# Two MLPs behind a decay attention: the second product into C11 ahead of U2's copy, and the first weights and gate tiles made sooner

## The chip, the core and the metric

The kernel runs on one core of a Trainium2 chip. The metric is the device time of one execution in microseconds (us). The engines of the core work at the same time, each through its own instructions in order: TensorE (PE; its weight loads are PEld), VectorE (DVE), ScalarE (ACT), GpSimd (POOL), and SyncE (SP), whose queue issues nearly all transfers here.

## The reference

```python
def _attn_ref(q, k, v, lam):          # 2 x 8 heads, 768 positions, 64 wide, in blocks of 64
    for b in range(nb):
        intra = np.einsum('bhic,bhjc->bhij', qb, kb) * Dmask[None]
        intra = np.einsum('bhij,bhjd->bhid', intra, vb)
        inter = np.einsum('bhid,bhde->bhie', qb * lam_pow[None], kv_state)
        out[:, :, sl] = intra + inter
        kv_state = lam_block * kv_state + np.einsum('bhsd,bhse->bhde', kb * rev_pow, vb)

def _moe_ref(x, w_in, w_out):         # x 1536 x 512, w_in 512 x 2048, w_out 2048 x 512
    h = x @ w_in
    return (h * np.cos(h)) @ w_out

def _moe2_ref(x, w_in, w_out):
    h = x @ w_in
    return (h * (1.0 / (1.0 + np.exp(-h)))) @ w_out
# out = moe2(moe(attention))
```

## The kernel before, in words

Three kinds of stage follow each other. **Attention** goes over six chunks of 128 positions (`c` 0 to 5) and leaves its result, transposed and already combined as the next stage wants it, in `xah`/`xal` (part A, the first 512 positions of both batches) and `xbh`/`xbl` (part B, the last 256). Then come, for layer 1 and again for layer 2, **the expansion** `gemm_in` (x @ w_in and the activation) and **the contraction** `gemm_out`/`gemm_outs` (@ w_out).

Every fp32 operand is split in two: `split` makes `hi` (a rounded copy, on ACT) and `lo` (the rest, `of - hi`, on POOL unless an engine is named). A product is made of hi*hi, lo*hi and hi*lo.

The expansion uses a scheme with seven products in place of eight. A *quad* is two row tiles of the hidden layer by two token halves; there are 16 per layer, eight of part A (512 columns) and eight of part B (256), in the order AA BB AB AB AB AB AA BB. `product(Q, i)` is six matmuls into one of three PSUM banks: products 1 and 2 into bank a (C11), 6, 5 and 3 into bank b, 7 and 4 into `d`. Banks a and b are the two halves of one tile, `cab`. Between them ACT copies: `copy_ab` (a to b after product 1), `copy_u(.., "u2")` (b after product 6, which is U2), `copy_u(.., "u4")` (b after product 5). DVE makes `h2` of d, u2 and u4 (`c22`, `c21`); ACT and DVE make the activation (`act_n`, `act_s`, `act_sin`, `act_g`; layer 2 needs only `act_n` and `act_g`), and SP stores the gate to DRAM (`gd`). The code is scheduled by hand: what is written order is each engine's order. The loop of `gemm_in` is skewed: round n starts quad n+1 (products 1, 7, 6, 2) and finishes quad n (5, 3, 4). Waits between engines are kept per tile.

In each round two numbered slots (2n and 2n+1) run `task`s, which prepare weights: `rebias_w` (ACT), `convert_w` (DVE), `load_next` (SP), `sum_w` (four sums of weights, POOL), `split_plain` and `split_sums`. For a pair of tiles they are `pair_tasks`; `w`, the converted tile, has four buffers. The last slots make the first w_out pieces (`out_tasks`), load the first gate tiles back (`load_g`) and split them (`prepare`).

The contraction goes over 16 hidden tiles f for three token blocks b: b = 0 and 1 interleaved, then b = 2. Its first matmuls stand in the last round of the expansion. While b = 2 of layer 1 runs, `keep_a` combines and splits the results of b = 0 and 1 as layer 2's part A, and layer 2's first two pairs of weights are made.

Of the kernel before, what the change touches and what calls it, by code (L numbers as in the profile page):

```python
# [8 lines left out]
F32 = mybir.dt.float32  # L9
# [4 lines left out]
ALU = mybir.AluOpType  # L14
PSUM = bass.MemoryType.PSUM
# [24 lines left out]
def tile_decay_attention__two_mlps(  # L40
# [84 lines left out]

    def sum_w(L, j):
        (wa0, wb0), (wa1, wb1) = (
            (w32[L, f, 0][:, 0:2 * P], w32[L, f, 0][:, 2 * P:]) for f in (2 * j, 2 * j + 1)
        )
        s = conv.tile([P, 4, 2 * P], F32, tag="S", name="S")  # L130
        for i, (x, y, op) in enumerate(
            ((wa1, wb1, ALU.add), (s[:, 0], wa0, ALU.subtract), (wa0, wa1, ALU.subtract), (wb0, s[:, 1], ALU.subtract))
        ):
            nc.gpsimd.tensor_tensor(out=s[:, i], in0=x, in1=y, op=op)  # L134
        sums[L, j] = s
# [19 lines left out]

    def pair_tasks(L, j):
        f = 2 * j
        return [
            lambda: rebias_w(L, f, 0),
            lambda: (rebias_w(L, f + 1, 0), convert_w(L, f, 0), load_next()),  # L160
            lambda: (convert_w(L, f + 1, 0), load_next(), sum_w(L, j)),
            lambda: split_plain(L, j),
            lambda: split_sums(L, j),
        ]
# [27 lines left out]
    )  # L192
    ps_o, ps_s = (psum_up.enter_context(tc.tile_pool(name=n, bufs=1, space=PSUM)) for n in ("ps_o", "ps_s"))
    half = [slice(e * C, (e + 1) * C) for e in range(2)]
# [181 lines left out]
    def att_l(c):  # L376
        h, l, ps, xc, t = xs.pop(c)
        nc.scalar.copy(h[:, 3:7], t)
        engine = nc.gpsimd if c < CA - 1 else nc.vector
        for o, x in ((slice(0, 2), xc[:, 0]), (2, xc[:, 1, 1])):  # L380
            engine.tensor_tensor(out=l[:, o], in0=x, in1=h[:, o].bitcast(F32), op=ALU.subtract)
        nc.gpsimd.tensor_tensor(out=l[:, 3:7], in0=t, in1=h[:, 3:7].bitcast(F32), op=ALU.subtract)

# [90 lines left out]
    def gemm_in(L, tasks, begun):  # L474

        qs = quads[L]

        def task(i):
            for x in tasks.get(i, []):
                x()  # L480

        if not begun:
            late = keep_b()
            late.pop(0)()
            product(qs[0], 1)
            copy_ab(qs[0])
            product(qs[0], 7)
            late.pop(0)()
            product(qs[0], 6)
            copy_u(qs[0], "u2")  # L490
            product(qs[0], 2)
            for i, x in enumerate(late):
                tasks.setdefault(i // 2, []).append(x)
        for n, Q in enumerate(qs):
            nxt = qs[n + 1] if n + 1 < len(qs) else None
            old = qs[n - 1] if n else None
            if nxt:
# [12 lines left out]
            if nxt:  # L510
                product(nxt, 7)
                product(nxt, 6)
            else:
                gemm_out(L, 0, 0, (0, 1))
            if old:
                act_g(old, 1)
            if nxt:
                copy_u(nxt, "u2")
            task(2 * n + 1)
            if nxt:  # L520
                product(nxt, 2)
# [29 lines left out]

    def prepare(L, b, f):
        if f >= FT or (L, b, f) in gt:
            return
        t = gf.pop((L, b, f))
        if b == 0:
            if L not in slab:
                slab[L] = [xpool.tile([P, SLOTS, 2, TB], F32R, tag=n, name=m) for n, m in (("xah", "gh"), ("xal", "gl"))]
            gh, gl = (x[:, f % SLOTS] for x in slab[L])
            split(gh, gl, t)  # L560
            for i in range(2):
                gt[L, i, f] = gh[:, i], gl[:, i]
        else:
            gh = tpool.tile([P, TB], F32R, tag="t2", name="gh", bufs=5)
            gl = tpool.tile([P, TB], F32R, tag="u", name="gl", bufs=3)
            split(gh, gl, t)
            gt[L, b, f] = gh, gl
# [36 lines left out]
    def keep_a():  # L604
# [65 lines left out]
    def gemm_outs(L, tasks):  # L670
# [3 lines left out]
        for b, f in items:  # L674
# [5 lines left out]
            if b == 1 and f >= FT - 4:  # L680
                load_g(L, 2, 2 * (f - FT + 4))
                if f >= FT - 2:
                    prepare(L, 2, f - FT + 2)
            if b == 2:
                if f >= 2 and f % 2 == 0:
                    load_g(L, 2, f + 4)
                prepare(L, 2, f + 2)
# [9 lines left out]
    with tc.manual_schedule():  # L697
# [29 lines left out]
        for c in range(SC):  # L727
# [31 lines left out]
            if c == 3:  # L759
                p0[0]()  # L760
            if c == 4:
                p0[1]()
            if c == 5:
                p0[2]()
# [4 lines left out]
                p0[3]()  # L769
            att_intra(c - 1)  # L770
# [5 lines left out]
        att_scores(c, 0, ps_s, "s")  # L776
        p0[4]()
        p1[0]()
        att_t(c - 1)
        product(first, 1)  # L780
        copy_ab(first)
        att_scores(c, 1, ps_s, "s")
        p1[1]()
        att_l(c - 1)
        product(first, 2)
        att_inter(c, ps_o, "o")
        product(first, 7)
# [20 lines left out]
        for L in range(2):  # L808
            tasks = {}
            for j in range(2, FP):  # L810
                place(tasks, min(4 * j - 8, 18), pair_tasks(L, j))
            for f, n in enumerate((20, 22, 24, 25, 26, 28, 29)):
                place(tasks, n - 1, out_tasks(L, f))
            for f, (n, m) in enumerate(((28, 29), (28, 30), (30, 31), (30, 32))):
                tasks.setdefault(n, []).append(lambda L=L, f=f: load_g(L, 0, f))
                if m < 32:
                    tasks.setdefault(m, []).append(lambda L=L, f=f: prepare(L, 0, f))
            gemm_in(L, tasks, L == 0)
# [4 lines left out]
            if L == 0:  # L823
# [43 lines left out]
```

## Time and profile before

| | |
|---|---|
| time, median of 3 runs | 654.67 us (650.4 to 656.73) |
| the profiled execution | 654.53 us, of which the span is 652.6 us |
| busy share of the span | PE 90%, DVE 55%, ACT 47%, POOL 55% |
| mean granted TensorE clock | 0.961 of full speed |
| TensorE's waits for ACT's copies u | 34.9 us in 32 waits |

A row of a trace gives the start and length of an operation (or a group of equal ones, `x4`), its output and inputs by the program's names, and in square brackets how long its engine stood idle before it and what ended that. L410 is the line of `product`, L432 that of `copy_u`, L121 and L122 the two halves of `split`, L591 the contraction.

### The profile page before, as it was taken

What the parts mean: (1) busy time and instruction counts of PE and PEld (TensorE: products, weight loads), DVE (VectorE), ACT (ScalarE), POOL (GpSimd) and SP (SyncE); (2) the same over time, 40 slices, a digit from 0 to 9 for tenths busy, and PEclk for the clock granted to TensorE, in tenths of its full rate; (3) what the DMA queues carried; (4) which work ended last, traced back from release to release, by engine and by line L of the source; (5) the groups of instructions that cost most, each with busy time, mean ns of one, the idle gap of its engine ahead of it and who ended that gap; (6) DMA issues with size and microseconds to landing.
All of it is one profiled execution on the core that took longest, in us unless ns stands there. A gap on an engine that the chain in (4) does not pass through costs nothing.

```text
span 652.6 us, 8744 instructions
## 1 busy us (share of the span) xinstructions
PE 586.1 (90%) x3313; PEld 482.2 (74%) x3313; DVE 360.8 (55%) x387; ACT 307.8 (47%) x482; POOL 356.1 (55%) x267
## 2 busy tenths in 40 slices
PE   7997887888788879999998998888889799999996
PEld 4876676777667768888886777777768688888884
DVE  5677766576786766960194046565676479502101
ACT  4565456666667465530364265554565455301210
POOL 3676724355372258990279635455672689821441
PEclk9998997898979779999998999999999799999999
DMA  9995234244343558771115015344555787304401
GB/s 180 211 215 141 65 130 133 93 162 160 131 161 130 195 209 283 247 247 43 34 55 172 0 33 209 115 161 159 180 190 194 277 289 260 96 1 138 157 29 64
DMA packets 79225, 97.04 MB, mean 149 GB/s; under 512 B 40784, under 2 KB 57168, under 8 KB 79184
## 3 DMA queue, kind: packets, MB, share of 16 engines
q1 hardware_dynamic: 76944, 95.96, 45.9%
q10 hardware_dynamic: 2240, 0.53, 0.4%
q8 instruction: 26, 0.43, 0.3%
q14 instruction: 15, 0.12, 0.1%
HBM read 68.16 MB, written 28.31 MB: 148 GB/s over the span
## 4 chain that ended last, share of the span: by engine, by line
PE 67%; ACT 11%; POOL 6%; DVE 5%; DMA 5%; issue 3%; SPq 1%; ACTq 0%; POOLq 0%; DVEq 0%
PE y L591 37%; PE cab L410 21%; PE d L410 8%; ACT u L432 3%; ACT s L465 2%; DMA v<-in_v_dram 2%; POOL win L122 2%; POOL S L134 2%; ACT win L121 2%; ACT s L449 2%; POOL gl L122 1%; DMA gf<-gd 1%; DVE w L116 1%; DMA q<-in_q_dram 1%; DVE sb L115 1%
## 5 line engine op out<-in xcount | busy, mean ns | idle before, releaser
L122 POOL TENSOR_TENSOR gl<-gf,gh 128x1024 fp32r<-128x1024 f32 (+1 forms) x64 | 122.4, 1918 | 98.6 <-ACT gh L121 73.9
L591 PE MATMUL y<-wout,gh 128*128 128x512 f32 x384 | 119.7, 394 | 4.0 <-ACT gh L121 2.3
L591 PE MATMUL y<-gh,wout 128*128 128x512 f32 x384 | 120.5, 396 | 2.2 <-ACT gh L121 2.2
L410 PE MATMUL cab<-xah,win 128*128 128x512 f32 x320 | 93.8, 416 | 14.3 <-ACT u L432 11.7
L116 DVE SCALAR_TENSOR_TENSOR w<-w,sb 128x512 uint32<-128x512 uint32 x64 | 90.3, 1411 | 20.0 <-ACT w L106 14.0
L121 ACT CAST gh<-gf 128x1024 fp32r<-128x1024 f32 (+1 forms) x64 | 52.9, 831 | 98.6 <-PE y L591 35.8
L591 PEld LDWEIGHTS y<-wout,gh 128*128 128x128 f32 x384 | 72.5, 190 | 19.6 <-ACT gh L121 2.6
L591 PEld LDWEIGHTS y<-gh,wout 128*128 128x128 f32 x384 | 73.5, 192 | 17.4 <-ACT gh L121 2.4
L410 PEld LDWEIGHTS cab<-xah,win 128*128 128x128 f32 x320 | 59.1, 196 | 32.5 <-ACT u L432 18.5
L134 POOL TENSOR_TENSOR S<-w 128x256 f32<-128x256 f32 x32 | 33.8, 1056 | 87.8 <-DVE w L116 87.8
L591 PE MATMUL y<-gl,wout 128*128 128x512 f32 x192 | 76.7, 399 | 5.5 <-POOL gl L122 5.5
L410 PE MATMUL cab<-xbh,win 128*128 128x256 f32 x320 | 57.1, 303 | 26.3 <-ACT u L432 23.2
L591 PE MATMUL y<-wout,gl 128*128 128x512 f32 x192 | 75.8, 395 | 1.7 <-POOL gl L122 1.7
L122 POOL TENSOR_TENSOR wout<-w,wout 128x512 fp32r<-128x512 f32 x32 | 50.8, 1589 | 42.0 <-ACT wout L121 42.0
L410 PEld LDWEIGHTS cab<-xbh,win 128*128 128x128 f32 x320 | 48.7, 201 | 33.4 <-ACT u L432 26.5
L115 DVE TENSOR_SCALAR sb<-raw 128x512 uint32<-128x512 uint32 x64 | 67.8, 1059 | 0.7
L122 POOL TENSOR_TENSOR win<-S,win 128x512 fp32r<-128x512 f32 x32 | 45.8, 1452 | 15.8 <-ACT win L121 15.8
L440 DVE TENSOR_TENSOR h<-d,u 128x512 f32<-128x512 f32 (+1 forms) x32 | 17.8, 556 | 64.7 <-PE d L410 64.7
L410 PE MATMUL cab<-xal,win 128*128 128x512 f32 x160 | 51.5, 404 | 0.0
L666 DVE COPY o<-y 128x512 f32<-128x512 f32 x12 | 8.1, 689 | 77.3 <-PE y L591 75.1
L591 PEld LDWEIGHTS y<-gl,wout 128*128 128x128 f32 x192 | 36.7, 191 | 15.1 <-POOL gl L122 7.4
L106 ACT ACTIVATE w<-raw 128x512 f32<-128x512 f32 x64 | 42.8, 669 | 7.8 <-POOL win L122 7.8
(113 smaller groups left out, 926.4 us busy)
## 6 DMA issues: line engine op xcount, KB each, us to landing
gf<-gd SPq DMA_DIRECT2D x48, 512.0 KB, 4.7
raw<-in_moe_w_in_dram SPq DMA_DIRECT2D x32, 512.0 KB, 3.9
gd<-s SPq DMA_DIRECT2D x32, 512.0 KB, 2.9
raw<-in_moe_w_out_dram SPq DMA_DIRECT2D x32, 512.0 KB, 3.5
gd<-s SPq DMA_DIRECT2D x32, 256.0 KB, 2.0
v<-in_v_dram SPq DMA_DIRECT2D x12, 256.0 KB, 6.5
out_dram<-o SPq DMA_DIRECT2D x12, 256.0 KB, 2.0
k<-in_k_dram SPq DMA_DIRECT2D x6, 256.0 KB, 6.0
```

What stands on the lines that cost most here:

```text
L106: nc.scalar.activation(w, raw[piece][:, :, 1].bitcast(F32), AF.Prelu, scale=2.0**-112, alpha=-(2.0**32))
L115: nc.vector.tensor_scalar(out=sb, in0=r[:, :, 0], scalar1=2.0**-29, scalar2=7.0, op0=ALU.mult, op1=ALU.min)
L116: nc.vector.scalar_tensor_tensor(out=w, in0=w, scalar=3, in1=sb, op0=ALU.logical_shift_left, op1=ALU.bitwise_or)
L121: nc.scalar.copy(hi, of)
L122: (engine or nc.gpsimd).tensor_tensor(out=lo, in0=of, in1=hi.bitcast(F32), op=ALU.subtract)
L134: nc.gpsimd.tensor_tensor(out=s[:, i], in0=x, in1=y, op=op)
L410: nc.tensor.matmul(Q.banks[bank], w[:, part, wu, kt * P:(kt + 1) * P], x[:, xu, kt, :], start=start and m == 0 and kt == 0, stop=m == 2 an ...
L432: nc.scalar.copy(t, Q.banks["b"])
L440: nc.vector.tensor_tensor(out=Q.h2[:, 0], in0=Q.banks["d"], in1=Q.u2, op=ALU.add)
L449: nc.scalar.activation(t, source(Q, i), AF.Identity, scale=1.0 / (2.0 * math.pi), bias=quarter)
L465: nc.scalar.activation(t, t, AF.Sin, scale=2.0 * math.pi, bias=half_pi)
L591: nc.tensor.matmul(y[m], x, z, start=f == 0 and n == 0, stop=f == FT - 1 and n == 2)
```

## The change

In `gemm_in`, `product(nxt, 2)` is written before `copy_u(nxt, "u2")`. `load_g(L, 0, 0)` goes to the head of round 14, and the first three gate tiles are split in two pieces (`prepare(.., 2)`). At the end of the attention the first weights are converted one chunk sooner, summed and split ahead of x's lo; x's lo of chunk 3 goes to POOL, that of chunks 4 and 5 reads PSUM, and a late part of it is issued after the second pair's sums. The two PSUM pools `ps_o` and `ps_s` change places. At the end of layer 1's contraction all four subtractions of `rest` and the sums of weights run on DVE, the weights' tasks start at f = 0, and the gate loads of b = 2 stand one step later at first and then two steps ahead. Loop counts, arithmetic and tile sizes stay.

```diff
-    def sum_w(L, j):
+    def sum_w(L, j, engine):
...
-    def pair_tasks(L, j):
+    def pair_tasks(L, j, engine=nc.gpsimd):
...
-            lambda: (convert_w(L, f + 1, 0), load_next(), sum_w(L, j)),
+            lambda: (convert_w(L, f + 1, 0), load_next()),
+            lambda: sum_w(L, j, engine),
...
-        engine = nc.gpsimd if c < CA - 1 else nc.vector
-        for o, x in ((slice(0, 2), xc[:, 0]), (2, xc[:, 1, 1])):
+        engine, x = (nc.gpsimd, xc) if c < CA else (nc.vector, ps)
+        for o, x in ((slice(0, 2), x[:, 0]), (2, x[:, 1, 1])):
             engine.tensor_tensor(out=l[:, o], in0=x, in1=h[:, o].bitcast(F32), op=ALU.subtract)
...
             product(qs[0], 6)
+            product(qs[0], 2)
             copy_u(qs[0], "u2")
-            product(qs[0], 2)
...
+            if n == len(qs) - 2:
+                load_g(L, 0, 0)
             if nxt:
                 product(nxt, 1)
...
             if nxt:
+                product(nxt, 2)
                 copy_u(nxt, "u2")
             task(2 * n + 1)
-            if nxt:
-                product(nxt, 2)
             product(Q, 3)
...
             for i in range(2):
                 gt[L, i, f] = gh[:, i], gl[:, i]
+                if pieces == 2:
+                    split(*gt[L, i, f], t[:, i])
+            if pieces == 1:
+                split(gh, gl, t)
...
-            split(h[:, 3 + i], l[:, 3 + i], t[i], nc.vector if i % 2 else nc.gpsimd)
+            split(h[:, 3 + i], l[:, 3 + i], t[i], nc.vector)
...
             if b == 2:
-                if f >= 2 and f % 2 == 0:
-                    load_g(L, 2, f + 4)
+                if f % 2 == 0:
+                    load_g(L, 2, f + 6)
...
+            if c == 5:
+                p0[3]()
+                p0[4]()
             if c > 1:
                 att_l(c - 2)
...
-                for j, ns in enumerate(((3, 4, 5, 7, 8), (8, 9, 10, 11, 12))):
-                    for n, x in zip(ns, pair_tasks(1, j)):
+                for j, ns in enumerate(((0, 1, 2, 3, 7, 8), (4, 5, 6, 9, 10, 12))):
+                    for n, x in zip(ns, pair_tasks(1, j, nc.vector)):
```

TensorE in a middle round of layer 1, before: product 6 of a part A quad (`cab_1226`), its product 2, and product 3 of the part B quad ahead of it (`cab_1149`).

```order
L410 MATMUL cab_1226<-xah_309,win_1119 128x512 [waits Activation_49]
L410 MATMUL cab_1226<-xah_309,win_1119 128x512 x3
L410 MATMUL cab_1226<-xal_310,win_1119 128x512 x2
L410 MATMUL cab_1226<-xah_309,win_1119 128x512 [waits Activation_49]
L410 MATMUL cab_1226<-xah_309,win_1119 128x512 x3
L410 MATMUL cab_1226<-xal_310,win_1119 128x512 x2
L410 MATMUL cab_1149<-xbh_836,win_962 128x256 x4
L410 MATMUL cab_1149<-xbl_837,win_962 128x256 x2
```

The same three products in the changed kernel.

```order
L414 MATMUL cab_1226<-xah_309,win_1125 128x512 [waits Activation_49]
L414 MATMUL cab_1226<-xah_309,win_1125 128x512 x3
L414 MATMUL cab_1226<-xal_310,win_1125 128x512 x2
L414 MATMUL cab_1226<-xah_309,win_1125 128x512 x4
L414 MATMUL cab_1226<-xal_310,win_1125 128x512 x2
L414 MATMUL cab_1149<-xbh_836,win_961 128x256 [waits Activation_49]
L414 MATMUL cab_1149<-xbh_836,win_961 128x256 x3
L414 MATMUL cab_1149<-xbl_837,win_961 128x256 x2
```

Product 2 waits for nothing now, and the wait for an ACT copy stands at product 3, whose copy is u4.

SP at the end of layer 1's expansion, before: stores of the gate, a load of raw weights, and the first two gate tiles (`gf`).

```order
L472 DMA gd0_74<-s_2032 128x1024 [waits DVE_49]
L472 DMA gd0_74<-s_2100 128x1024 [waits DMAHW3_49,DVE_49]
L92 DMA raw_2138<-in_moe_w_out_dram 128x1024 [waits DMAHW4_49,DMAHW5_49,DVE_49,Activation_49]
L545 DMA gf_2142<-gd0_74 128x1024 [waits DMAHW2_49,PE_49]
L545 DMA gf_2144<-gd0_74 128x1024 [waits DMAHW6_49,DVE_49]
```

The same place after.

```order
L476 DMA gd0_74<-s_2032 128x1024 [waits DVE_49]
L550 DMA gf_2113<-gd0_74 128x1024 [waits DMAHW3_49,DMAHW2_49,PE_49]
L476 DMA gd0_74<-s_2100 128x1024 [waits DMAHW4_49,DVE_49]
L92 DMA raw_2140<-in_moe_w_out_dram 128x1024 [waits DMAHW5_49,DVE_49,Activation_49]
L550 DMA gf_2144<-gd0_74 128x1024 [waits DMAHW6_49,DVE_49]
```

The first gate tile is two entries further ahead in the queue; the second stays where it was.

POOL where the attention ends, as a difference: lo of the first pair's plain weights, lo of x (`xal`, `xbl`), and lo of the sums.

```order
 L122 TENSOR_TENSOR win<-w,win 128x512
 L122 TENSOR_TENSOR win<-w,win 128x256
+L382 TENSOR_TENSOR xal<-xc,xah 128x4x128
+L382 TENSOR_TENSOR xal<-xc,xah 128x2x128
+L383 TENSOR_TENSOR xal<-xt,xah 128x8x128
 L122 TENSOR_TENSOR win<-S,win 128x512 x2
-L382 TENSOR_TENSOR xbl<-xt,xbh 128x8x128
 L134 TENSOR_TENSOR S<-w 128x256
```

The weights' lo now stands ahead of x's lo of chunk 3, and one lo of part B goes behind the second pair's sums.

## Rows read from the trace of the kernel before

**Rows 1.** Busy time by stretch: start:end, length, PE, PEld, DVE, ACT, POOL, clock, DMA, GB/s.

```profile
82.00:223.00 141.00, 116.61 (x590) 98.09 (x589) 94.53 (x118) 92.17 (x146) 58.86 (x53) 0.92 0.40 138
223.00:240.00 17.00, 12.80 (x54) 10.72 (x55) 10.84 (x13) 8.00 (x14) 8.18 (x5) 0.70 0.83 279
...
372.00:504.00 132.00, 118.93 (x640) 99.50 (x639) 78.61 (x99) 74.25 (x132) 65.75 (x57) 1.00 0.43 150
504.00:519.00 15.00, 10.70 (x51) 8.80 (x52) 6.89 (x9) 6.24 (x10) 9.38 (x5) 0.77 0.84 297
327.00:372.00 45.00, 41.16 (x173) 33.25 (x172) 23.11 (x16) 19.34 (x31) 40.35 (x31) 0.96 0.26 82
```

**Rows 2.** Waits, whole span: waiting engine <- releaser: us, times, longest.

```profile
PE cab L410 <- ACT u L432: 34.9, 32, 3.3
...
ACT u L432 <- PE cab L410: 23.1, 22, 2.3
```

**Rows 3.** Chain that ended last, layer 2: start, length of one product (x6).

```profile
392.03 0.73 PE d L410 x6
...
437.10 1.36 PE d L410 x6
```

**Rows 4.** Timeline of TensorE, layer 2: product 2 of three successive quads.

```profile
443.95 1.19 PE L410 MATMUL cab<-xah,win 128*128 128x512 f32 x4 [0.68 <-ACT u L432]
...
451.75 0.74 PE L410 MATMUL cab<-xbh,win 128*128 128x256 f32 x4 [1.16 <-ACT u L432]
...
460.95 1.19 PE L410 MATMUL cab<-xah,win 128*128 128x512 f32 x4 [0.68 <-ACT u L432]
```

**Rows 5.** Timeline of TensorE, layer 1: product 2 of two part B quads.

```profile
140.47 0.74 PE L410 MATMUL cab<-xbh,win 128*128 128x256 f32 x4 [1.77 <-ACT u L432]
...
158.05 0.74 PE L410 MATMUL cab<-xbh,win 128*128 128x256 f32 x4 [1.76 <-ACT u L432]
```

**Rows 6.** Busy time in one pair of quads of layer 1.

```profile
140.00:158.00 18.00, 15.15 (x84) 12.91 (x84) 13.01 (x17) 13.04 (x23) 9.43 (x10) 1.00 0.42 146
```

**Rows 7.** Groups in 82 to 223: count, busy, mean ns, idle before them, releaser.

```profile
L449 ACT ACTIVATE s<-h,consts 128x1024 int32<-128x1024 f32 x8 | 9.2, 1153 | 9.5 <-DVE h L440 9.5
...
L440 DVE TENSOR_TENSOR h<-d,u 128x512 f32<-128x512 f32 x8 | 5.5, 692 | 21.2 <-PE d L410 21.2
...
L428 ACT COPY cab<-cab 128x256 f32<-128x256 f32 x8 | 2.9, 366 | 0.0
```

**Rows 8.** Timeline, layer 1, around 175 us.

```profile
175.31 0.67 ACT L106 ACTIVATE w<-raw 128x512 f32<-128x512 f32 x1 [4.71 <-POOL win L122]
...
177.49 0.74 PE L410 MATMUL cab<-xbh,win 128*128 128x256 f32 x4 [2.32 <-ACT cab L428]
```

**Rows 9.** Timeline at the passage from expansion to contraction, layer 1, then 2.

```profile
229.03 1.04 ACT L121 CAST gh<-gf 128x1024 fp32r<-128x1024 f32 x1 [4.50 <-DMA gf<-gd]
...
230.13 0.73 PE L591 MATMUL y<-gh,wout 128*128 128x512 f32 x2 [2.17 <-ACT gh L121]
...
232.57 0.79 PE L591 MATMUL y<-gl,wout 128*128 128x512 f32 x1 [1.71 <-POOL gl L122]
...
509.74 0.73 PE L591 MATMUL y<-wout,gh 128*128 128x512 f32 x2 [2.35 <-ACT gh L121]
```

**Rows 10.** Timeline of SP and TensorE late in layer 1's contraction.

```profile
340.28 0.96 SPq L548 DMA_DIRECT2D gf<-gd  x2
...
348.77 0.50 PE L591 MATMUL y<-gl,wout 128*128 128x512 f32 x1 [3.23 <-POOL gl L122]
```

**Rows 11.** Timeline of TensorE at the end of the attention.

```profile
61.82 0.73 PE L410 MATMUL cab<-xah,win 128*128 128x512 f32 x2 [2.17 <-POOL win L122]
...
79.59 0.73 PE L410 MATMUL d<-xah,win 128*128 128x512 f32 x2 [0.31 <-POOL win L122]
```

**Rows 12.** Timeline of DVE, end of layer 1: two subtractions of one size.

```profile
323.05 1.23 DVE L596 TENSOR_TENSOR T<-y,x 128x1024 f32<-128x1024 f32 x1 [35.49 <-ACT b L613]
...
327.01 2.30 DVE L596 TENSOR_TENSOR T<-x,T 128x1024 f32<-128x1024 f32 x1
```

More of the change, by code (lines that the diff above doesn't have):

```diff
@@ L133, in sum_w @@
         ):
-            nc.gpsimd.tensor_tensor(out=s[:, i], in0=x, in1=y, op=op)
+            engine.tensor_tensor(out=s[:, i], in0=x, in1=y, op=op)
         sums[L, j] = s
@@ L192, in tile_decay_attention__two_mlps @@
     )
-    ps_o, ps_s = (psum_up.enter_context(tc.tile_pool(name=n, bufs=1, space=PSUM)) for n in ("ps_o", "ps_s"))
+    ps_s, ps_o = (psum_up.enter_context(tc.tile_pool(name=n, bufs=1, space=PSUM)) for n in ("ps_s", "ps_o"))
     half = [slice(e * C, (e + 1) * C) for e in range(2)]
@@ L378, in att_l @@
         nc.scalar.copy(h[:, 3:7], t)
-        engine = nc.gpsimd if c < CA - 1 else nc.vector
-        for o, x in ((slice(0, 2), xc[:, 0]), (2, xc[:, 1, 1])):
+        engine, x = (nc.gpsimd, xc) if c < CA else (nc.vector, ps)
+        for o, x in ((slice(0, 2), x[:, 0]), (2, x[:, 1, 1])):
             engine.tensor_tensor(out=l[:, o], in0=x, in1=h[:, o].bitcast(F32), op=ALU.subtract)
-        nc.gpsimd.tensor_tensor(out=l[:, 3:7], in0=t, in1=h[:, 3:7].bitcast(F32), op=ALU.subtract)
+        late = lambda: nc.gpsimd.tensor_tensor(out=l[:, 3:7], in0=t, in1=h[:, 3:7].bitcast(F32), op=ALU.subtract)
+        if c == CA:
+            return late
+        late()
     class Quad:
@@ L550, in load_g, with prepare @@
                 gf[L, 2, f + i] = t[:, i]
-    def prepare(L, b, f):
+    def prepare(L, b, f, pieces=1):
         if f >= FT or (L, b, f) in gt:
@@ L559, in prepare @@
             gh, gl = (x[:, f % SLOTS] for x in slab[L])
-            split(gh, gl, t)
             for i in range(2):
                 gt[L, i, f] = gh[:, i], gl[:, i]
+                if pieces == 2:
+                    split(*gt[L, i, f], t[:, i])
+            if pieces == 1:
+                split(gh, gl, t)
         else:
@@ L680, in gemm_outs @@
             if b == 1 and f >= FT - 4:
-                load_g(L, 2, 2 * (f - FT + 4))
+                if f >= FT - 3:
+                    load_g(L, 2, 2 * (f - FT + 3))
                 if f >= FT - 2:
@@ L759, in tile_decay_attention__two_mlps @@
             if c == 3:
-                p0[0]()
+                rebias_w(0, 0, 0)
+                convert_w(0, 0, 0)
+                load_next()
             if c == 4:
-                p0[1]()
+                rebias_w(0, 1, 0)
+                convert_w(0, 1, 0)
+                load_next()
             if c == 5:
-                p0[2]()
                 qk_pools.close()
@@ L768, in tile_decay_attention__two_mlps @@
                 )
-                p0[3]()
             att_intra(c - 1)
@@ L776, in tile_decay_attention__two_mlps @@
         att_scores(c, 0, ps_s, "s")
-        p0[4]()
+        p0[5]()
         p1[0]()
         att_t(c - 1)
+        late = att_l(c - 1)
         product(first, 1)
@@ L783, in tile_decay_attention__two_mlps @@
         p1[1]()
-        att_l(c - 1)
         product(first, 2)
@@ L789, in tile_decay_attention__two_mlps @@
         p1[2]()
+        p1[3]()
         att_x(c)
-        p1[3]()
+        p1[4]()
         product(first, 6)
+        late()
         att_t(c)
-        p1[4]()
+        p1[5]()
         att_l(c)
@@ L810, in tile_decay_attention__two_mlps @@
             for j in range(2, FP):
-                place(tasks, min(4 * j - 8, 18), pair_tasks(L, j))
+                at_n = min(4 * j - 8, 18)
+                p = pair_tasks(L, j)
+                for n, x in zip((0, 1, 2, 2, 3, 4), p):
+                    tasks.setdefault(at_n + n, []).append(x)
             for f, n in enumerate((20, 22, 24, 25, 26, 28, 29)):
@@ L816, in tile_decay_attention__two_mlps @@
                 if m < 32:
-                    tasks.setdefault(m, []).append(lambda L=L, f=f: prepare(L, 0, f))
+                    tasks.setdefault(m, []).append(lambda L=L, f=f: prepare(L, 0, f, 2))
             gemm_in(L, tasks, L == 0)
```

## The prediction

> **What bounds the kernel now.** I first read the busy time by stretch [rows 1]. TensorE has the most work in every stretch, so the question is what it loses, and that is of two kinds. One is idle time: 24.4 us of the 141 in layer 1's expansion (141 - 116.61), 13.1 of 132 in layer 2's, 4.2 and 4.3 in the two passages to the contraction, 3.8 at the end of layer 1's contraction. The other is the granted clock, which has two levels, 1.2 and 2.4 GHz: a mean of 0.92 over 141 us means that 0.08 x 141 = 11.3 us of full-speed work was not done; the passages lose 0.30 x 17 = 5.1 and 0.23 x 15 = 3.5, the end of layer 1's contraction 0.04 x 45 = 1.8. Layer 2's expansion ran at 1.00. Next the table of waits [rows 2]: of TensorE's idle time 34.9 us in 32 waits is for a copy u. The timeline shows where: at product 2 of each quad, for U2's copy [rows 4, 5]. Nothing in the arithmetic asks for that. Product 2 adds to bank a, U2 is read from bank b, but both are one tile, and a write written after a read of its tile waits for it.
>
> **The main edit: product 2 ahead of U2's copy.** Product 2 now waits for nothing; the copy waits for product 2 instead of 6, and product 3 waits for u4 itself. At full clock a product lasts 1.36 us in part A and 0.73 in part B [rows 3], so a pair of quads is 7 x 2.09 = 14.6 us of TensorE. In layer 2 a pair takes 460.95 - 443.95 = 17.0 us [rows 4]: 0.68 + 1.16 = 1.84 of wait and 0.5 of starting again, a quarter us each time (four matmuls took 1.19 behind the wait). In layer 1 it takes 158.05 - 140.47 = 17.6 [rows 5].
>
> What is late next? Queued behind U2's copy on ACT are the weights' tasks of the odd slot and act_n, which waits for product 3 anyway; u2 itself is wanted by c21 after product 4. So the copy has time. The tight place is copy_ab of a part B quad, wanted by product 6. From the end of product 4 of the part A quad ahead, DVE's c21 takes 0.69, act_n of h2 1.15, the copy 0.37 [rows 7], with about 0.1 at each of three hand-overs some 2.5; TensorE meanwhile has products 1, 5 and 7, 0.73 + 1.36 + 0.73 = 2.82. It fits by 0.3. The whole pair must also fit: ACT is busy 13.04 and DVE 13.01 of the 18 us that hold one pair of layer 1 [rows 6], against 14.6. ACT's wait for h2 costs it 9.5 / 8 = 1.2 in a part A quad [rows 7], so ACT is full at 14.3 or a little over. I take 15.2 for a pair of layer 1, and 14.8 in layer 2, where the 132 us hold 74.3 of ACT work.
>
> One stall stays: where the first w_out piece is rebiased, ACT stood 4.71 us until POOL freed a `w`, act_n stood behind it, and TensorE waited 2.32 for copy_ab [rows 8]. POOL's work there is unchanged and TensorE comes sooner by the u2 waits it no longer has; I take 4.5 in layer 1 and 1.5 in layer 2, and in layer 1 a fall of the clock behind it, 3 us.
>
> The sums. Layer 1 loses 24.4 + 11.3, and 14 new starts of a quarter us, 39 in all. Left over: 6 pairs x 0.6, the stall 4.5, clock 3, some 4 for the first quads and the weights' arrival: 15. Gain **24** (with all left over doubled 9, with only the pairs' 3.6 and 3 more 32). Layer 2 loses 13.1 + 16 quarters = 17; left over 8 pairs x 0.2 and the stall 1.5, say 3. Gain **14** (10 to 16).
>
> **The passages.** The first gate tile came late: ACT waited 4.50 us for it, TensorE 2.17 for hi and 1.71 for lo [rows 9]. Now its load stands ahead of a store that waits for DVE, and the split comes in halves, so the first matmuls need half of each. But the load is not all. POOL has a w_out piece to split before the first half and another between the first and second tile, and the second tile's load has not moved. With 9.3 lost in layer 1's passage and 7.8 in layer 2's, 5 and 4 may stay. Gain **4** and **4** (1 to 6 each). Behind the moved load SP holds a store that needs DVE anyway; it costs nothing.
>
> **End of layer 1's contraction.** The gate load for f = 6 left SP only at 340.28, behind raw weights, and TensorE waited 3.23 for its lo [rows 10]. Now the load is ahead of them, and POOL loses two subtractions and eight sums. Lost there 3.8 + 1.8; gain **4** (0 to 5.6). What takes the load is DVE, busy 23.1 of 45 us [rows 1]. Two subtractions of 1.23 alone [rows 12] and eight sums, for which there is no DVE row (at most 0.69 each, the 512-wide row in [rows 7], as they are 256 wide), are 8 us: 31 of 45.
>
> A subtraction with both inputs in SBUF took 2.30 beside POOL where one from PSUM took 1.23 [rows 12]. The Trainium skill (SBUF — State Buffer, Who interferes with whom) says that a DVE instruction with two SBUF inputs and a GpSimd instruction that reads SBUF shut each other out for a whole instruction. It speaks against this move: by it, with 1.1 more for each of ten, DVE would stand at 42 of 45 us and this gain would be near 0; by the plain rows it is 4.
>
> **Start.** TensorE waited 2.17 us for POOL's lo of the first weights [rows 11]. They are ready sooner now. But lo of part B goes ahead of the second pair's sums on POOL, and there TensorE waited already [rows 11], so what is gained at 62 us is mostly given back at 79. Gain **1** (-1 to 3).
>
> 24 + 14 + 4 + 4 + 4 + 1 = 51 from the profiled execution's 654.5 (the median is 654.7, the same) gives **603 us**.
>
> **Rivals.**
> - *The clock stays up in layer 1 and the stall stays small.* The gain there is 32, and 2 more in each passage: 591. For it: layer 2 has 1.00 with waits up to 1.2 us. Against it: the stall of rows 8 is ACT's and POOL's, not U2's.
> - *ACT and DVE bound layer 1.* Pairs stay at 16.6, because the two engines' hand-overs do not close up: 6 x 1.4 = 8 less, and the clock falls as often as before for another 6: 617. For it: 13.0 of 14.6 on both engines. Against: ACT still waited 23.1 us for products ahead of its copies u [rows 2], time that it can give.
> - *The change does not do what it says.* The wait goes from product 2 to 3, for u4, or to 5, for u2. Only the other terms are left, 13 less some: 643. Against: u4 is copied ahead of the slot's tasks, and three products lie between.
> - *Slower: ACT pays for product 2.* If ACT has no time to spare, each u2 copy comes one product later and everything behind it too: 8 x 2.09 per layer, 33 us, less the 13 of the other terms: 675. It decides where ACT's spare time per pair, 17.6 - 13.0 = 4.5, falls below its waits for h2 plus 2.09. These are 1.2 and less for part B; so it should not.
>
> **How the numbers follow.** Chances: forecast 0.62 (own range 595 to 613), clock stays up 0.13, ACT and DVE bound 0.17, wait only moved 0.05, slower 0.03. The range of 590 to 622 takes in the second and third with their spread and leaves out the last two and the tails. One per cent (6.5 us) is what a measurement of this kernel can tell from no change: faster 0.95, same 0.02, slower 0.03.
>
> **What would show it.** The wait PE cab <- ACT u falls from 34.9 us to under 6. ACT's own waits for cab before u rise. A middle pair takes 15.2 in layer 1 and 14.8 in layer 2. The wait of ACT for POOL's win at the first w_out piece is still there, and TensorE's wait behind it has grown. The gate's first hi no longer waits for a DMA, but its lo still waits for POOL. No wait of 3 us in layer 1's last block. I am wrong if pairs of layer 1 stay above 16, or if TensorE's clock there does not rise above 0.95.

## The result, and the profile after

The changed kernel takes 615.08 us (median of 4 runs, 610.88 to 615.33) beside 654.44 for the kernel before in the same session: a ratio of 0.939, 95% interval 0.933 to 0.945. The profiled execution took 614.86 us, its span is 613.1. The forecast was 603; the time lies in the range given (590 to 622), but above the forecast's own range (595 to 613). It is beside the rival that gave 617, by luck: that rival has 14 us less of layer 1's expansion, and the expansion gave nearly what was forecast (22.2 for 24). What is missing is elsewhere.

First a table by stretch, from TensorE's timeline in one trace of each kernel. An expansion ends here with product 5 of its last quad, the passage with that quad's product 4.

| stretch | before, us | after, us | gain | forecast |
|---|---|---|---|---|
| to product 6 of layer 1's second quad | 80.62 | 81.71 | -1.1 | 1 |
| from there to the end of layer 1's expansion | 147.34 | 125.09 | 22.2 | 24 |
| passage of layer 1 | 11.03 | 12.09 | -1.1 | 4 |
| layer 1's contraction | 133.73 | 129.54 | 4.2 | 4 |
| layer 2's expansion | 134.67 | 121.17 | 13.5 | 14 |
| passage of layer 2 | 11.29 | 9.54 | 1.8 | 4 |
| the rest | 133.9 | 134.0 | 0 | 0 |

The sum is 39.5 where 51 was forecast. The table of waits of the changed kernel (who waits, for whom, us in total, times, longest) answers to [rows 2]:

```profile
ACT u L436 <- PE cab L414: 42.1, 24, 4.6
...
DVE xt L371 <- POOL xbl L383: 10.2, 1, 10.2
PE cab L414 <- ACT cab L432: 9.5, 7, 3.3
...
PE cab L414 <- ACT u L436: 6.3, 2, 5.0
```

TensorE's 34.9 us for copies u are 6.3 (under 6 was forecast), and two waits are left of 32, 5.00 at the start and 1.31 in layer 1's passage; ScalarE waits for the products instead, as it should. The second line is new. Busy time by stretch answers to [rows 1] and [rows 6] (layer 1's expansion, its middle pair, its passage, layer 2's expansion, its passage):

```profile
82.00:207.00 125.00, 113.78 (x618) 96.69 (x618) 97.98 (x118) 91.80 (x148) 63.19 (x54) 0.97 0.48 164
137.60:153.77 16.17, 15.17 (x84) 12.91 (x84) 13.46 (x17) 12.31 (x21) 9.32 (x8) 1.00 0.48 164
207.00:219.00 12.00, 7.90 (x25) 5.83 (x26) 7.39 (x10) 5.23 (x10) 8.75 (x6) 0.72 0.91 307
348.00:470.00 122.00, 119.23 (x663) 103.58 (x661) 82.49 (x101) 73.48 (x133) 67.64 (x58) 0.99 0.48 165
470.00:479.00 9.00, 6.42 (x25) 4.59 (x26) 3.17 (x6) 4.08 (x8) 6.72 (x5) 0.81 1.01 382
```

The clock in layer 1's expansion went from 0.92 to 0.97. In both passages TensorE is still idle for about a third of the time (busy 7.90 of 12 and 6.42 of 9 us) and at a low clock (0.72 and 0.81). Four places in the timeline of the changed kernel say where the missing 11.5 us are. The start, on GpSimd, VectorE, ScalarE and TensorE in turn (start, length, in brackets the idle time ahead and who ended it):

```profile
70.82 2.34 POOL L383 TENSOR_TENSOR xbl<-xt,xbh 128x1024 fp32r<-128x1024 f32 x1
...
73.19 0.69 DVE L371 TENSOR_TENSOR xt<-pso,xc 128x512 f32<-128x512 f32 x1 [10.21 <-POOL xbl L383]
...
75.79 0.58 ACT L436 COPY u<-cab 128x512 f32<-128x512 f32 x1
...
76.42 2.07 PE L414 MATMUL cab<-xah,win 128*128 128x512 f32 x4 [5.00 <-ACT u L436]
```

`xt` has one buffer. The subtraction that the change moved behind product 6 still reads it, so VectorE stands 10.21 us ahead of its next `att_t` (over 4 of them it would have waited anyway, for ScalarE's copy `xc`, which ended at 67.33), and a chain of three engines ends at TensorE, which then runs its four matmuls in 2.07 instead of 1.2. TensorE had been 3.7 us ahead (its first product at 55.10, before at 58.84), and this takes all of it. How much of the 3.7 is the change's is open: the run with the main edit alone, whose attention is that of the kernel before, has its first product at 56.95, and runs with the changed kernel's attention have it at 54.76 to 57.23.

A middle pair of layer 1, the same engines:

```profile
137.61 1.18 PE L414 MATMUL d<-xah,win 128*128 128x512 f32 x4 [0.76 <-DVE h L444]
...
141.81 0.42 DVE L115 TENSOR_SCALAR sb<-raw 128x512 uint32<-128x512 uint32 x1
142.33 0.69 DVE L116 SCALAR_TENSOR_TENSOR w<-w,sb 128x512 uint32<-128x512 uint32 x1
...
149.21 1.07 PE L414 MATMUL d<-xah,win 128*128 128x512 f32 x4
...
149.35 3.23 POOL L122 TENSOR_TENSOR win<-S,win 128x512 fp32r<-128x512 f32 x2
...
149.91 1.52 DVE L115 TENSOR_SCALAR sb<-raw 128x512 uint32<-128x512 uint32 x1
151.53 1.59 DVE L116 SCALAR_TENSOR_TENSOR w<-w,sb 128x512 uint32<-128x512 uint32 x1
153.04 0.68 DVE L444 TENSOR_TENSOR h<-d,u 128x512 f32<-128x512 f32 x1
...
153.75 1.15 ACT L453 ACTIVATE s<-h,consts 128x1024 int32<-128x1024 f32 x1 [2.65 <-DVE h L444]
...
153.78 1.19 PE L414 MATMUL d<-xah,win 128*128 128x512 f32 x4 [0.96 <-DVE h L444]
```

Product 4 was in bank d at about 150.7, but c21 (L444), which reads it there, came at 153.04, and product 7, the last line, needs the bank. A weight's conversion (L115, L116) stands ahead of c21 on VectorE and took 3.1 us beside GpSimd's two subtractions, where the pair's other conversion took 0.42 + 0.69. This pair is 153.78 - 137.61 = 16.17 us; the two ahead of it take 16.34 and 15.53. In layer 2 it is 14.61, TensorE's own work:

```profile
404.51 1.07 PE L414 MATMUL d<-xah,win 128*128 128x512 f32 x4
...
419.12 1.07 PE L414 MATMUL d<-xah,win 128*128 128x512 f32 x4
```

Layer 1's first w_out piece, which answers to [rows 8], and its passage, which answers to [rows 9]:

```profile
164.89 0.67 ACT L106 ACTIVATE w<-raw 128x512 f32<-128x512 f32 x1 [4.40 <-POOL win L122]
...
167.06 0.74 PE L414 MATMUL cab<-xbh,win 128*128 128x256 f32 x4 [3.35 <-ACT cab L432]
...
169.07 1.91 PE L414 MATMUL cab<-xah,win 128*128 128x512 f32 x4
...
206.91 1.54 POOL L122 TENSOR_TENSOR wout<-w,wout 128x512 fp32r<-128x512 f32 x1 [5.95 <-ACT wout L121]
208.42 3.14 POOL L122 TENSOR_TENSOR gl<-gf,gh 128x512 fp32r<-128x512 f32 x2
...
209.91 0.50 PE L599 MATMUL y<-gl,wout 128*128 128x512 f32 x1 [1.77 <-POOL gl L122]
...
210.33 0.41 DVE L444 TENSOR_TENSOR h<-d,u 128x256 f32<-128x256 f32 x1
...
210.77 0.72 ACT L453 ACTIVATE s<-h,consts 128x512 int32<-128x512 f32 x1 [2.32 <-DVE h L444]
...
212.42 1.22 PE L414 MATMUL cab<-xbh,win 128*128 128x256 f32 x4 [1.31 <-ACT u L436]
...
470.74 1.14 ACT L121 CAST gh<-gf 128x512 fp32r<-128x512 f32 x2 [2.37 <-DMA gf<-gd]
471.41 0.93 PE L599 MATMUL y<-wout,gh 128*128 128x512 f32 x2 [1.81 <-ACT gh L121]
```

The first stall is there as forecast, 3.35 us. In the passage the tile itself is no longer late in layer 1; its lo waits behind a w_out piece on GpSimd, and product 3 waits for a u4 that stands on ScalarE behind another late c21, again behind a conversion of 3.1 us (207.23 to 210.40). In layer 2 ScalarE still waits for the load (2.37).

### The profile page after: what moved, and what is told of

It is laid out like the page before. It is cut to its first block, busy times and chain, and to the rows that moved or that the text cites. A ratio compares the mean times of both kernels' runs of the same rounds, so it can differ in the third digit from the quotient of the medians.

```text
span 613.1 us, 8757 instructions
## 1 busy us (share of the span) xinstructions
PE 572.3 (93%) x3312; PEld 474.8 (77%) x3313; DVE 366.4 (60%) x395; ACT 305.0 (50%) x488; POOL 355.2 (58%) x265
## 4 chain that ended last, share of the span: by engine, by line
PE 68%; ACT 7%; DVE 7%; POOL 6%; issue 5%; DMA 5%; ACTq 0%; SPq 0%; POOLq 0%; DVEq 0%
PE y L599 41%; PE cab L414 16%; PE d L414 7%; DMA v<-in_v_dram 2%; DVE s L475 2%; DVE w L116 2%; DVE sb L115 2%; POOL win L122 2%; POOL gl L122 2%; POOL S L134 2%; ACT s L453 1%; DMA q<-in_q_dram 1%; ACT s L469 1%; PE psc L325 1%; ACT s L457 1%
## 5 line engine op out<-in xcount | busy, mean ns | idle before, releaser
L122 POOL TENSOR_TENSOR gl<-gf,gh 128x512 fp32r<-128x512 f32 (+1 forms) x70 | 128.8, 1848 | 94.8 <-ACT gh L121 70.0
L116 DVE SCALAR_TENSOR_TENSOR w<-w,sb 128x512 uint32<-128x512 uint32 x64 | 92.5, 1446 | 15.2 <-ACT w L106 9.3
L414 PE MATMUL cab<-xah,win 128*128 128x512 f32 x320 | 91.4, 408 | 9.0 <-ACT u L436 5.0
L121 ACT CAST gh<-gf 128x512 fp32r<-128x512 f32 (+1 forms) x70 | 53.5, 775 | 92.7 <-DMA gf<-gd 34.6
L134 POOL TENSOR_TENSOR S<-w 128x256 f32<-128x256 f32 x28 | 31.1, 1110 | 71.1 <-DVE w L116 71.1
L115 DVE TENSOR_SCALAR sb<-raw 128x512 uint32<-128x512 uint32 x64 | 67.1, 1049 | 0.7
L414 PE MATMUL cab<-xbh,win 128*128 128x256 f32 x320 | 53.8, 291 | 8.4 <-ACT cab L432 7.0
L414 PEld LDWEIGHTS cab<-xbh,win 128*128 128x128 f32 x320 | 46.8, 193 | 12.6 <-ACT cab L432 8.5
L122 POOL TENSOR_TENSOR win<-S,win 128x512 fp32r<-128x512 f32 x32 | 48.0, 1520 | 9.7 <-ACT win L121 9.7
L436 ACT COPY u<-cab 128x512 f32<-128x512 f32 (+1 forms) x64 | 30.2, 472 | 42.2 <-PE cab L414 42.1
```

The costliest lines, as they stand in the source:

```text
L115: nc.vector.tensor_scalar(out=sb, in0=r[:, :, 0], scalar1=2.0**-29, scalar2=7.0, op0=ALU.mult, op1=ALU.min)
L116: nc.vector.scalar_tensor_tensor(out=w, in0=w, scalar=3, in1=sb, op0=ALU.logical_shift_left, op1=ALU.bitwise_or)
L121: nc.scalar.copy(hi, of)
L122: (engine or nc.gpsimd).tensor_tensor(out=lo, in0=of, in1=hi.bitcast(F32), op=ALU.subtract)
L134: engine.tensor_tensor(out=s[:, i], in0=x, in1=y, op=op)
L414: nc.tensor.matmul(Q.banks[bank], w[:, part, wu, kt * P:(kt + 1) * P], x[:, xu, kt, :], start=start and m == 0 and kt == 0, stop=m == 2 an ...
```

## Experiments

All times stand beside the kernel before on the same chip (654.3 to 654.6; 650.5 for the late load). Lengths of stretches, in us, from TensorE's timeline in one trace each; "expansion 1" runs from product 1 of the first quad.

| run | median | ratio, 95% interval | expansion 1 | passage 1 | contraction 1 | expansion 2 | passage 2 |
|---|---|---|---|---|---|---|---|
| before | 654.4 | | 169.1 | 11.03 | 133.7 | 134.7 | 11.29 |
| after | 615.1 | 0.939 (0.933 to 0.945) | 151.7 | 12.09 | 129.5 | 121.2 | 9.54 |
| main edit alone | 622.2 | 0.951 (0.948 to 0.953) | 149.8 | 14.17 | 133.8 | 121.1 | 12.77 |
| whole splits | 617.7 | 0.947 (0.943 to 0.951) | 149.2 | 14.24 | 129.2 | 121.2 | 13.04 |
| late load | 616.4 | 0.946 (0.942 to 0.950) | 150.5 | 13.48 | 128.5 | 121.1 | 10.53 |
| gate first | 611.4 | 0.936 (0.931 to 0.940) | 150.2 | 11.13 | 128.7 | 121.2 | 9.39 |
| lo at once | 607.4 | 0.928 (0.925 to 0.931) | 143.6 | 12.09 | 129.0 | 121.5 | 9.85 |
| c21 first | 612.9 | 0.937 (0.934 to 0.939) | 147.6 | 11.67 | 128.6 | 121.4 | 11.26 |
| w_out a slot later | 606.9 | 0.927 (0.924 to 0.930) | 148.0 | 11.99 | 128.5 | 118.4 | 9.85 |
| these three | 595.3 | 0.911 (0.907 to 0.915) | 137.5 | 11.53 | 129.8 | 117.3 | 10.67 |
| three, gate first | 593.5 | 0.908 (0.904 to 0.912) | 135.6 | 9.93 | 128.6 | 117.4 | 9.00 |
| these, u4 first | 593.8 | 0.910 (0.906 to 0.913) | 137.2 | 9.89 | 129.0 | 117.4 | 9.25 |
| sums on GpSimd | 619.8 | 0.949 (0.944 to 0.954) | 150.5 | 12.09 | 135.1 | 121.1 | 9.39 |
| old loads | 616.8 | 0.945 (0.941 to 0.949) | 150.8 | 12.09 | 130.6 | 121.2 | 10.59 |

Beside the changed kernel's interval only the main edit alone, lo at once, w_out a slot later and the three combined kernels stand clear; for the others the intervals do not part the time from the changed kernel's, and the stretches are read. Those vary too: where the code of a stretch is the changed kernel's, layer 2's passage took 9.39 to 10.59 and layer 1's contraction 128.5 to 129.8.

**The main edit alone.** In the kernel before:

```
+            if nxt:
+                product(nxt, 2)
                 copy_u(nxt, "u2")
             task(2 * n + 1)
-            if nxt:
-                product(nxt, 2)
```

and the same swap in the prologue.

> The kernel before with the main edit alone: product 2 ahead of U2's copy, in the prologue of a layer and in every round; nothing else of the change. Theory (the main edit is worth what the two expansions lost: the changed kernel's expansions are 22 and 13.5 us shorter): about 620 us, TensorE's waits for a copy u under 8 us, layer 1's middle pair at 16.2 and layer 2's at 14.8 as in the changed kernel. Rival (the earlier start and the split of the sums into a task of their own carry a part of the gain): 628 or more, middle pair of layer 1 above 16.6.

It took 622.18 us, 32.4 of the 39.4 that the whole change gives, and the theory holds: TensorE's waits for a copy u are 0.2 us, a middle pair takes 16.16 in layer 1 and 14.61 in layer 2. So the 6.3 us of the changed kernel came in with its other edits. Layer 1's expansion ends at 206.74 us, in the changed kernel at 206.80: in these two traces everything else that the change does before that point is worth nothing (runs with the same code up to there end it at 203.9 to 207.6). But the passages are longer than before the change, 14.17 for 11.03 and 12.77 for 11.29. Layer 1's, on SP, ScalarE and TensorE:

```profile
205.82 1.78 SPq L544 DMA_DIRECT2D gf<-gd  x2
...
211.35 1.04 ACT L121 CAST gh<-gf 128x1024 fp32r<-128x1024 f32 x1 [4.58 <-DMA gf<-gd]
...
212.45 1.22 PE L590 MATMUL y<-gh,wout 128*128 128x512 f32 x2 [5.71 <-ACT gh L121]
```

TensorE is there sooner and the tile is not. Its wait for hi grew from 2.17 us [rows 9] to 5.71. Of the gain in the expansions 3.1 and 1.5 us are given back here, before any edit of the passage has done anything.

**The passages: halves, load, order.** Three runs take one thing from the changed kernel, or add one. Whole splits:

```
-                    tasks.setdefault(m, []).append(lambda L=L, f=f: prepare(L, 0, f, 2))
+                    tasks.setdefault(m, []).append(lambda L=L, f=f: prepare(L, 0, f))
```

> The changed kernel, but the first gate tiles of an expansion's end are split whole again (one copy and one subtraction over both halves); their load stays early. Theory (the halves bring the first gl about 1.1 us sooner, the early load does the rest: with the main edit alone the passages took 14.17 and 12.77 us, in the changed kernel 12.09 and 9.54): passages of about 13.2 and 10.6, 616 to 618. Rival (the load alone did it, halves cost what they save): passages as in the changed kernel, 614 to 616.

Late load:

```
-            if n == len(qs) - 2:
-                load_g(L, 0, 0)
```

> The changed kernel, but the first gate tile's load at an expansion's end is issued where the kernel before had it; the splits in halves stay. With the load early and the split whole the passages took 14.24 and 13.04 us, as with the main edit alone (14.17 and 12.77). Theory (each of the two needs the other: the halves bring nothing while the tile itself comes at 211 us): passages of 13.5 to 14.5 and 12 to 13, 618 to 620. Rival (the halves alone do it): 12.1 and 9.5 as in the changed kernel, 614 to 616.

Neither theory nor rival had the passages right in either run, though 617.65 lies in the first theory's range. With the early load and whole splits the passages are as long as with neither edit (14.24 and 13.04); the load moves the wait from hi to lo and no more:

```profile
204.95 0.73 PE L599 MATMUL y<-gh,wout 128*128 128x512 f32 x2 [1.03 <-ACT gh L121]
208.10 0.50 PE L599 MATMUL y<-gl,wout 128*128 128x512 f32 x1 [2.42 <-POOL gl L122]
```

Halves with the late load, where TensorE waits 5.52 us for hi, give 13.48 and 10.53, and both edits 12.09 and 9.54. So in layer 1 each edit needs the other (0.7 and -0.1 alone, 2.1 together); in layer 2 the halves alone bring 2.2 of 3.2, and the rest is no more than that passage varies by.

Gate first:

```
+            for f, (n, m) in enumerate(((28, 29), (28, 30), (30, 31), (30, 32))):
...
             for f, n in enumerate((20, 22, 24, 25, 26, 28, 29)):
                 place(tasks, n - 1, out_tasks(L, f))
-            for f, (n, m) in enumerate(((28, 29), (28, 30), (30, 31), (30, 32))):
...
```

> The changed kernel, but in the slots at the end of an expansion the first gate tiles' splits stand ahead of the w_out tasks of the same slot (slots 29 to 31), where they stood behind them. Theory (in layer 1's passage two things wait: gl for a w_out piece on GpSimd, 1.54 us, and behind it product 3 for u4's copy, which ScalarE makes after act_n of an h2 that c21 gave late): the 1.77 us wait for gl goes below 0.4, the wait for u4 grows from 1.31 to about 2.5, so the whole gains 1.5 us at most: 613 to 615. Rival (gl alone is what holds the passage): both waits go, 611 or less.

The wait for u4 grew to 2.74 as the theory had it; lo still waited 0.96 us, and passage 1 lost 0.96. The median, 611.44, lies between the two theories, the passage accounts for about 1 of its 3.6, and the intervals do not tell this run from the changed kernel.

```profile
207.79 0.50 PE L599 MATMUL y<-gl,wout 128*128 128x512 f32 x1 [0.96 <-POOL gl L122]
...
211.73 1.22 PE L414 MATMUL cab<-xbh,win 128*128 128x256 f32 x4 [2.74 <-ACT u L436]
```

**The start: lo of chunk 4 at once.**

```
-        late = att_l(c - 1)
+        att_l(c - 1)()
...
-        late()
```

> The changed kernel, but GpSimd's subtraction for lo of chunk 4 (the four derived operands) is issued at once and not after product 6 of the first quad. Theory (it holds the only buffer xt, for which VectorE waited 10.21 us and TensorE then 5.00 at half clock behind it): product 5 of the first quad starts at 71 to 72 us in place of 76.42, at full clock; 6 to 9 us less, 606 to 609. Rival (the first weights' sums on GpSimd or the copies on ScalarE are late next, so the wait changes its name only): product 5 at 74 or later, at most 2 us less.

It is 7.7 us less, as the theory had it. VectorE's `att_t` is not held up, and product 5 starts at 72.34, at full clock, though TensorE was 1.2 us later than in the changed kernel at its first product:

```profile
68.14 0.69 DVE L371 TENSOR_TENSOR xt<-pso,xc 128x512 f32<-128x512 f32 x1 [3.06 <-ACT xc L358]
...
72.34 1.19 PE L414 MATMUL cab<-xah,win 128*128 128x512 f32 x4 [0.22 <-ACT u L436]
```

**Layer 1's pairs: c21 ahead of the conversion.** The conversion gets a task of its own behind c21 in the odd slots; the lists of slots change with it and are not shown.

```
             c21(Q)
+            task(2 * n + 1.5)
             act_n(Q, 1)
...
-            lambda: (rebias_w(L, f + 1, 0), convert_w(L, f, 0), load_next()),
+            lambda: rebias_w(L, f + 1, 0),
+            lambda: (convert_w(L, f, 0), load_next()),
```

> The changed kernel, but in every odd slot the conversion of a weight (sb and w on VectorE) is issued behind c21 of the round, not ahead of it; the rebias on ScalarE stays where it is. Theory (the order on VectorE holds layer 1's pairs: a conversion stretched to 3.1 us stands ahead of c21, so d and h2 come late): the wait of product 7 for h goes from 0.96 us to under 0.3, ScalarE's wait for h2 from 2.65 to under 1, the middle pair from 16.17 to about 15.2, the passage of layer 1 loses its 1.31 us wait for u4; all in all 6 to 8 us less than the changed kernel, 607 to 609. Rival (VectorE and ScalarE are full over the pair, whatever stands first): the conversion is late instead, the pair stays at 16.2, 613 to 616.

The mechanism is right. Product 7 of the middle pairs comes after 14.61 and 14.87 us and waits for nothing, c21 waits for product 4 (0.69) and no longer for a conversion, which comes one place later:

```profile
133.39 0.69 DVE L445 TENSOR_TENSOR h<-d,u 128x512 f32<-128x512 f32 x1 [0.69 <-PE d L415]
134.00 1.40 DVE L115 TENSOR_SCALAR sb<-raw 128x512 uint32<-128x512 uint32 x1
...
135.28 1.07 PE L415 MATMUL d<-xah,win 128*128 128x512 f32 x4
...
135.50 0.69 DVE L116 SCALAR_TENSOR_TENSOR w<-w,sb 128x512 uint32<-128x512 uint32 x1
...
150.15 1.42 PE L415 MATMUL d<-xah,win 128*128 128x512 f32 x4
...
164.24 1.01 PE L415 MATMUL cab<-xbh,win 128*128 128x256 f32 x3 [5.11 <-ACT cab L433]
```

The conversion also became cheaper there, 1.40 + 0.69 and in the next pair 0.76 + 1.60, as it meets less of GpSimd's work; the run does not part the two effects. But the whole took 612.93, the rival's number. Expansion 1 is only 4.1 us shorter, since TensorE now waits 5.11 at the first w_out piece in place of 3.35, and layer 2's passage is 1.7 longer, with the clock at half for more of it. The first product also came 2.1 us later, at 57.23, in a stretch that this edit does not touch.

**The first w_out piece one slot later.**

```
-            for f, n in enumerate((20, 22, 24, 25, 26, 28, 29)):
+            for f, n in enumerate((21, 22, 24, 25, 26, 28, 29)):
```

> The changed kernel, but the three tasks of the first w_out piece stand one slot later in both layers, so that its rebias comes behind product 5's copy and not ahead of act_n. Theory (ScalarE stood 4.40 us there for a buffer w that GpSimd had not yet freed, and act_n and copy_ab stood behind it): the 3.35 us wait of TensorE in layer 1 and the half clock behind it go, the 1.88 us wait in layer 2 goes; 5 to 7 us less, 608 to 610. Rival (a wait for the same buffer one slot later holds up the copies there): the same 3 us wait 2 us later, 613 to 616.

8.2 us less, more than the theory had. The 3.35 us wait at copy_ab and the 1.88 in layer 2 are gone, and waits of 2.12 and 0.87 for c21 follow in their place; expansion 1 is 3.7 and expansion 2 is 2.8 us shorter.

**Together.** All three edits (in one kernel), then with the gate first, then with u4's copy ahead of the old quad's sine in the last round:

> The three single edits together: conversions of odd slots behind c21, lo of chunk 4 at once, tasks of the first w_out piece one slot later. Theory (the 5 us that the first of these saved in layer 1's pairs were mostly waited away at the first w_out piece, 5.11 us in place of 3.35, which the third takes away): the three gains come in full, 615.1 - 7.7 - 8.2 - 6 = 593. Rival (the gains only add as measured): 615.1 - 7.7 - 8.2 - 2.2 = 597 or more.

> The three edits together and the gate tiles' splits ahead of the w_out tasks. Theory (with c21 early, u4's copy no longer holds product 3, so now the earlier gl counts): 2 to 4 us less than without the last edit, no wait over 0.7 in layer 1's passage, no half clock behind it. Rival (the w_out pieces, split later, are waited for in place of gl): the same time within 1 us.

```
-            if old:
+            if old and nxt:
                 act_sin(old, 0)
             product(Q, 5)
             copy_u(Q, "u4")
+            if old and not nxt:
+                act_sin(old, 0)
```

> The version with the four edits together, but in the last round of an expansion ScalarE makes u4's copy ahead of the sine of the old quad. Theory (product 3 of the last quad waits 2.42 us for a copy that stands behind that sine, and the sine waits for VectorE): that wait goes below 1, at most 0.5 of it comes back at the second gate tile: 1 to 2 us less, 591.5 to 592.5. Rival (the sine, later, gives the last gate store and so the next gate tile late): the same time, 593 to 595.

The three give 595.31, 19.8 less than the changed kernel where the single gains, 7.7, 2.2 and 8.2, add to 18.1. The median lies between the two expectations, so the conversions' part did not come in full; expansion 1 lost 14.2. Gate first takes another 1.8, which the intervals do not separate from nothing, but both passages are 1.6 us shorter: 593.49, the fastest kernel here. Its passage 1 still has a wait of 2.42 for u4, which was expected to be gone; moving u4's copy there ended that wait and made one of 1.84 at the second gate tile, and the time did not move, as the rival had it:

```profile
194.38 0.50 PE L603 MATMUL y<-gl,wout 128*128 128x512 f32 x1 [0.75 <-POOL gl L122]
198.22 0.73 PE L603 MATMUL y<-gh,wout 128*128 128x512 f32 x2 [1.84 <-ACT gh L121]
```

**The end of layer 1's contraction.** Sums and two subtractions back on GpSimd, loads as in the changed kernel; then the loads as before, the sums on VectorE:

```
-            split(h[:, 3 + i], l[:, 3 + i], t[i], nc.vector)
+            split(h[:, 3 + i], l[:, 3 + i], t[i], nc.vector if i % 2 else nc.gpsimd)
...
-                    for n, x in zip(ns, pair_tasks(1, j, nc.vector)):
+                    for n, x in zip(ns, pair_tasks(1, j)):
```

> The changed kernel, but at the end of layer 1's contraction the eight sums and two of the subtractions are on GpSimd again; the gate's loads stay early. Theory (the earlier load is what took the 3.2 us wait away; GpSimd's relief only keeps it small): the block's waits for gl stay under 1 us, 614 to 616. Rival (GpSimd would still be late with gl): a wait of 1.5 to 3 us is back there, 617 to 619.

```
-                if f >= FT - 3:
-                    load_g(L, 2, 2 * (f - FT + 3))
+                load_g(L, 2, 2 * (f - FT + 4))
...
-                if f % 2 == 0:
-                    load_g(L, 2, f + 6)
+                if f >= 2 and f % 2 == 0:
+                    load_g(L, 2, f + 4)
```

> The changed kernel, but the gate's loads around the end of a contraction are issued where the kernel before had them; sums and subtractions stay on VectorE. Theory (now that the run with GpSimd in their place took 5.6 us more in this contraction, GpSimd's relief is what counts): contraction of layer 1 at 129 to 131 us in place of 129.54, 614 to 617. Rival (both are needed): a wait of 2 to 3 us is back, contraction at 132 or more, 618.

My theory for the first fell, and the rival's price was too low: the contraction is 5.6 us longer and a wait of 3.62 is back, though the load was early. GpSimd makes a lo of the next layer's operand, four sums and then two gate tiles, and TensorE waits:

```profile
321.97 3.13 POOL L122 TENSOR_TENSOR gl<-gf,gh 128x512 fp32r<-128x512 f32 x2
...
323.46 0.58 PE L599 MATMUL y<-gl,wout 128*128 128x512 f32 x1 [3.62 <-POOL gl L122]
```

With the old loads and VectorE the contraction takes 130.6: the loads are worth 1.1 us there, hardly more than it varies by.

## Why the prediction was right and where it was not

**The main edit** was right: the wait at product 2 went (34.9 us to 0.2 with this edit alone), and the terms 24 and 14 measured 22.2 and 13.5. With this edit alone expansion 2 gives all of its 13.5, and expansion 1 ends where the changed kernel's does.

**Pairs of layer 1** were mis-sized: 16.17 us where 15.2 was said, and the text called that a sign of being wrong. The step that failed is the chain behind product 4, where c21 was given 0.69 right after it. A conversion of 3.1 us stands between them. The rival had ScalarE and VectorE bound layer 1 with pairs of 16.6, as their hand-overs do not close up. One hand-over does not, but the engines are not full, 12.31 and 13.46 of 16.17, and with c21 ahead the same work takes 14.61 to 14.87. The term still came out near 24, in part because misses offset each other. Of the 39 us, 17 are left over and not 15: the stall 3.35 for 4.5, the clock 0.03 x 125 = 3.8 for 3, one wait of 2.1 in the first quads for 4, and so some 8 in the pairs for 3.6.

**The passages** are the largest miss: 4 and 4 measured -1.1 and 1.8, 7.3 of the 11.5 us. The failed step is that they were priced by what the trace of before lost there. The main edit alone brings TensorE to layer 1's passage 21.2 us sooner, and the tile, whose load stands behind stores in SP's queue, only 17.7 (ScalarE's first copy at 211.35 for 229.03 [rows 9]); so the loss there grew first, by 3.1 and 1.5. The edits give 2.1 and 3.2 back. The prediction named the load first; by itself it gave nothing.

**The start** is the second miss: -1.1 for 1. The size says little, as the same old code put product 6 of the second quad at 80.62 us in one trace and 82.12 in another (main edit alone); the wait of 5.00 and the 7.7 us that its removal gave do. The step looked at GpSimd's order alone, and had that order wrong: the deferred subtraction goes behind the second pair's sums and ahead only of their lo. Which buffer it holds by being late was not asked.

**The end of the contraction** measured 4.2 for 4, and for a reason the text gave second place: GpSimd's relief, not the load, is what counts. VectorE was busy for 34.6 of 45 us, almost without a break from 303.99 to 339.1, between the 31 and the 42 of the prediction. A sum of 256 columns alone, and one beside GpSimd's lo, in the changed kernel:

```profile
319.64 0.42 DVE L134 TENSOR_TENSOR S<-w 128x256 f32<-128x256 f32 x1
...
332.82 3.70 POOL L122 TENSOR_TENSOR gl<-gf,gh 128x512 fp32r<-128x512 f32 x2
...
333.86 1.50 DVE L134 TENSOR_TENSOR S<-w 128x256 f32<-128x256 f32 x1
```

The Trainium skill (SBUF — State Buffer, Who interferes with whom) says that a VectorE instruction with two SBUF inputs and a GpSimd instruction that reads SBUF exclude each other; the 1.50 beside 0.42 agrees. By the prediction's reading of it the gain would have been near 0; it was 4.2, since TensorE first needed the operands at 348.43. The same section of the Trainium skill names tensor_scalar among the operations that can take the shared port pair, and the conversion's first half, 1.52 us beside GpSimd and 0.42 without, agrees. That the sharing is what stretches them is read from such rows; no run here took GpSimd's work away to show it.

## What to carry to other kernels

When an edit makes the bounding engine faster, price the next stage's first input again: it may come through a queue that gains less (here 17.7 of 21.2 us), and then more is lost there than the old trace shows (14.17 us of passage for 11.03). Before an instruction is put off, ask whether its inputs lie in a single buffer that others wait for. In an engine's queue, put first what the bounding engine's chain waits for, and the work that only must be done sometime behind it: moving a few instructions in their queues gave another 21.6 us here (615.1 to 593.5) with the same work.

## What was not expected

The same waits cost differently. In the run with c21 first, TensorE's waits in layer 2's passage were 1.77 and 0.63 us, in the changed kernel 1.81, 0.43 and 0.62, yet the granted clock over the passage was 0.61 in the one and 0.82 in the other, and the passage took 11.26 for 9.54. What decides this is open.

And waits that were removed gave more than their own length. At the start 4.8 of the 5.00 us went, and the time fell by 7.7. The clock has most of the rest: behind the wait the changed kernel's products 5 and 7 take 5.29 us (76.42 to 81.71), with four matmuls in 2.07, and without it 2.87 (72.34 to 75.21). With the first w_out piece a slot later, 3.35 and 1.88 us of waits went, 2.12 and 0.87 came, and the two expansions are 6.5 us shorter; over 82 to 203 us the clock is 0.99 for 0.97, over 400 to 465 us 0.99 for 0.97, which is an estimated 2.4 and 1.3 us.
